# Other places in the order of issue for batches 2 to 8 of a linear-attention and leaky-ReLU kernel

## The chip, the cores and the metric

The kernel runs on one core of a Trainium2 chip. The metric is the device time of one execution in microseconds (us). Times before are the median of three runs; the profile is one further execution, taken by the hardware profiler.

## The reference

For each of 8 batches and 8 heads, with 576 positions of 64 features, `phi(x)` is `relu(x)` times a cosine and times a sine of the position, side by side (128 features). Then

```
kv  = phi(k)^T v            z   = sum over positions of phi(k)
num = phi(q) kv             den = phi(q) z + 1e-6
attn = num / den            x   = attn as (4608 tokens, 512)
h   = x @ w_in              (512 x 2048)
out = max(0.01 h, h) @ w_out    (2048 x 512)
```

Inputs and output are float32.

## The kernel before

**Groups.** 512 of a batch's 576 positions form one group of rows; the last 64 of all eight batches together form a ninth group. So there are groups 0 to 8, each with 512 rows, and each goes through attention and both layers. Operands of matmuls are float16, sums float32.

**Attention of a group.** `loads(b, 0/1/2)` bring q, k and v by SyncE's queue into staging buffers (pool `stage`, three buffers). `k_part`, `q_part` and `v_part` convert them on VectorE (DVE) or ScalarE (ACT): index `j` is a quarter of the rows (4 is the tail of 64), the next index is 0 for cosine and 1 for sine. `kv_all(b)` makes phi(k)^T v with 36 small matmuls and a copy on ACT; it reads `vmain` (from `v_part(b, 0)` for heads 0 to 3 and `v_part(b, 1)` for heads 4 to 7) and `vtail` (`v_part(b, 2)`). `q_transpose_dma(b, j)` transposes a quarter of phi(q) by a DMA. `num(b, j)` multiplies it with kv into the one buffer `ps_num` of its pool, and DVE divides by `den` into `xs`. `x_transpose_dma(b, j)` turns `xs` into a quarter of `xT` by a DMA; for group 2 alone `x_transpose(2, j)` does it on TensorE (PE), and ACT copies the result.

**Layers by seven products.** From group 1's second layer and group 2's first layer on, a 2 x 2 block product is made from seven block products instead of eight (Strassen's scheme). `x_sums(g, s)` makes the sums of blocks of `xT` that these need (tile `xw`): s = 1 gives `xw[0]`, s = 2 `xw[1]` (which product 6 reads), s = 3 and 4 the rest. `w1_sums` and `w2_sums` do so for the weights. `p1(g, t, n, ...)` is product n of row tile t in the first layer, four matmuls with 256 columns; `p2(g, n, pair, u, ...)` is one of the second layer, also four matmuls. Between products, ACT copies sums in PSUM from bank to bank (`seed`), ACT and DVE gather results (`u_copy`, `u_add`), and ACT applies the leaky ReLU (`lrelu`, `u_lrelu`). `g_sums(g, n, lo, hi)` makes on DVE the block sums for the second layer, and `o_copy`, `o_add`, `o_store` gather and store its output.

**Order.** The pool scheduler decides nothing here: instructions go to each engine's queue in the order in which the code issues them, and each queue runs strictly in order. From line 1008 on, the code collects steps with a position each in a list `line`, sorts the list by position and issues it. PE's products lie on a regular grid: `f1_stream(g)` places the first layer of group g at `top[g]`, with 58 positions to a group (56 from group 4 on), and `f2_stream(g - 1)` the second layer of the group before beside it, so that both alternate in runs of four matmuls. All other steps are put at positions from tables written out by hand:

- `AT[b]` for the attention of group b (5 stands for 5 to 8; from 4 on relative to `top[b]`), with entries `load`, `kc`, `ks`, `v`, `kv`, `qc`, `qs`, `qt`, `num`, `xt`, `xs`
- `ENG[b]` for the engine of each conversion
- `F1_AT`, `F4_AT`, `F2_AT`, `F24_AT` for the ACT and DVE steps behind each product
- `G1_AT`, `G_AT`, `G3_AT`, `G4_AT`, `GL_AT` for `g_sums`, `W1_AT`, `W2_AT`, `R_AT` for the sums of weights
- `LAST`, `LAG4` for where the last second layers begin

Everything before that (group 0, the attention of group 1, the conversion of the weights) is issued directly, ends near 52 us, and is not touched.

Of the kernel before, what the change touches and what calls it, by code (L numbers as in the profile page):

```python
# [18 lines left out]
def kernel(  # L19
# [60 lines left out]
    ACT, DVE, POOL = nc.scalar, nc.vector, nc.gpsimd  # L80
# [151 lines left out]
    kv = [const.tile([P, H, NE], dt.float16, name=f"kv{b}") for b in range(B)]  # L232
# [574 lines left out]

    SEED, JOIN, ALL = 2, 3, 4

    F1_AT = {'seed': (0.3, 0.7, 0.5), 'u1': (1.0, 1.0, 1.0), '11': (5.3, 1.3, 2.8), 'u2': (0.3, 0.7, 0.5), '22': (1.8, 0.6, 0.2), '21': (0.5, 0.8, 1.9), '12': (0.5, 1.6, 1.1), 'out': (2.7, 2.7, 2.1)}  # L810

    P_AT = (
# [4 lines left out]
    ONE_AT = ((4, 7), (12, 14), (17, 18), (22, 25))  # L817

    P4_AT = {1: 0, 6: 3, 2: 5, 7: 6, 5: 8, 4: 9, 3: 11}
    F4_AT = {'seed': 1.0, 'u1': 4.1, '11': 7.9, 'u2': 7.6, '22': 9.4, '21': 10.3, '12': 11.2, 'out': 12.9}  # L820

    def f1_stream(g):

        evs = [(-0.1, quarters, (g,))]
        for t in range(3 if g < ALL else 4):
# [7 lines left out]
            for n, nm, f, args in (  # L833
# [4 lines left out]
            ):  # L838
                pos_ = at_[n] + F1_AT[nm][t] if g < ALL else 7 * t + F4_AT[nm]
                evs.append((pos_, f, (g, *args)))  # L840
# [76 lines left out]
                o_src[o * TAIL : (o + 1) * TAIL, pairs, cols],  # L917
            )

    F24_AT = {'u0': 2.7, '11': -0.2, 'u1': 1.7, 'u2': -0.7, '22': 0.6, '21': 0.5, '12': 0.0, 'low': 1.9, 'top': 3.1}  # L920
    F2_AT = {'u0': 0.7, '11': -0.7, 'u1': -0.1, 'u2': -0.9, '22': -0.5, '21': -0.1, '12': 0.9, 'low': 2.5, 'top': 3.3}

    def f2_stream(g):

# [3 lines left out]
        for n, bank, fresh in (  # L928
# [7 lines left out]
            for nm, f, args in {  # L936
# [73 lines left out]
    def put(pos, f, *args):  # L1010
        line.append((pos, len(line), f, args))
# [4 lines left out]

    AHEAD, LAG, LAST, LAG4 = 14, 2, 9, 2.5
    length = {g: 58 if g < ALL else 56 for g in range(2, NG)}  # L1020
    top = {2: 2 * NFT + AHEAD}
    for g in range(3, NG + 1):
# [24 lines left out]

    W1_AT = {3: (38.5, 53.5)}  # L1050
# [22 lines left out]
    for i in range(2):  # L1073
        put(W1_AT[3][i], w1_sums, i, 3, 0, 4 - 2 * i)
    for s, at_ in zip((1, 2, 4, 3), R_AT):
        put(top[ALL - 1] + at_, w1_sums, 1, s, 2, 4)
    for s, at_ in W2_AT.items():
        for i in range(2 - len(at_), 2):
            put(at_[i - 2], w2_sums, i, s)
    for s, at_ in G1_AT.items():  # L1080
        for u in range(2):
            put(at_[u], g_sums, 1, s, 4 * u, 4 * u + 4)
    for g in range(2, NG):
        which = GL_AT if g == NG - 1 else G_AT if g < ALL - 1 else G3_AT if g < ALL else G4_AT
        for s, at_ in which.items():
# [58 lines left out]
```

## Time and profile before

| what | value |
|---|---|
| median of three runs | 271.71 us (271.64 to 272.72) |
| the profiled execution, device time | 272.88 us |
| its span, first to last instruction | 271.0 us |
| matmuls | 2660 |
| busy: PE, DVE, ACT | 263.2, 201.6, 200.8 us |
| granted TensorE clock | 0.999 |
| DMA: bytes moved, mean rate | 57.05 MB, 211 GB/s |
| last matmul ends | 267.4 us |

The busy times are shares of one execution. PE is matmul time and PEld is the time of loading weights, which runs beside it; the ends of matmuls are modelled, so the start of one to the start of the next is the better measure of what a matmul takes. A row of a timeline has the start in us, the time, the engine, the line, the operation and the tiles; "x4" says that four instructions stand in one row, and a bracket how long the engine was idle before and for whom it waited. All steps of one helper have one line, so a row is told by its tiles and its place in time.

### The profile page before, as it was taken

The numbers are of one execution on the slowest core, as the hardware profiler recorded it, in microseconds if no ns is written. First come the engines' busy times: TensorE is split into PE (matmuls) and PEld (weight loads), VectorE is DVE, ScalarE is ACT, GpSimd is POOL, SyncE is SP. The second block draws the span as 40 slices with busy tenths as digits, with TensorE's granted clock in tenths as the row PEclk, the third lists the DMA queues.
The fourth block names the chain that finished last, engine by engine and source line by source line (L and its number), as shares of the span: only waits on it lengthen the run. The fifth ranks groups of instructions, "written<-read, shape, count | busy, mean of one in ns | idle before, by whom it ended". The sixth has DMA issues, their size and how long they took to land.

```text
span 271.0 us, 6597 instructions
## 1 busy us (share of the span) xinstructions
PE 263.2 (97%) x2660; PEld 226.1 (83%) x2660; DVE 201.6 (74%) x445; ACT 200.8 (74%) x330; POOL 10.6 (4%) x21
## 2 busy tenths in 40 slices
PE   7799999999999999999999999999999999999994
PEld 5786455765888989889999999999999889999983
DVE  5774799797986797899779696979577758644652
ACT  6666556696878998798899789978966756766621
POOL 1055101000000000000000000000000000000000
PEclk9999999999999999999999999999999999999999
DMA  6999999998999869998999699969384412200324
GB/s 229 313 355 409 408 350 371 354 241 269 296 225 350 148 189 259 297 189 238 280 261 158 184 273 271 175 208 157 77 135 160 62 41 95 82 0 2 144 50 119
DMA packets 87150, 57.05 MB, mean 211 GB/s; under 512 B 56656, under 2 KB 82256, under 8 KB 86608
## 3 DMA queue, kind: packets, MB, share of 16 engines
q1 hardware_dynamic: 86816, 56.37, 78.8%
q8 instruction: 21, 0.34, 0.5%
q10 hardware_dynamic: 304, 0.26, 0.3%
q14 instruction: 9, 0.07, 0.1%
HBM read 36.70 MB, written 9.44 MB: 170 GB/s over the span
## 4 chain that ended last, share of the span: by engine, by line
PE 89%; DVE 4%; DMA 3%; ACT 3%; issue 1%; SPq 0%; DVEq 0%; ACTq 0%
PE ps_o L882 33%; PE ps_h L777 29%; PE ps_h L454 5%; PE ps_h L490 5%; PE ps_o L470 5%; PE ps_h L882 3%; PE ps_num L375 3%; DMA kst<-in_k_dram 3%; PE ps_kv L291 2%; ACT g L751 1%; DVE kpm L240 1%; DVE xp L391 1%; PE ps_qt L365 1%; PE ps_kvh L291 1%; PE ps_numh L411 1%
## 5 line engine op out<-in xcount | busy, mean ns | idle before, releaser
L882 PEld LDWEIGHTS <-g 128*128 128x128 f16 x640 | 62.5, 98 | 7.3 <-DVE g L251 0.2
L251 DVE TENSOR_TENSOR u<-ps_h,u 128x512 f32<-128x512 f32 x52 | 35.8, 688 | 25.2 <-PE ps_h L777 22.3
L882 PE MATMUL ps_o<-w,g 128*128 128x256 f16 x352 | 51.2, 273 | 0.0
L777 PEld LDWEIGHTS <-w 128*128 128x128 f16 x416 | 44.4, 114 | 1.2
L777 PE MATMUL ps_h<-xT,w 128*128 128x256 f16 x288 | 43.3, 273 | 0.0
L804 ACT ACTIVATE g<-u 128x1024 f16<-128x1024 f32 x26 | 27.5, 1057 | 10.9 <-DVE u L251 10.8
L777 PEld LDWEIGHTS <-wa 128*128 128x128 f16 x312 | 34.0, 113 | 1.7 <-DVE xw L254 0.6
L790 ACT ACTIVATE g<-ps_h 128x512 f16<-128x512 f32 x52 | 31.2, 602 | 5.7 <-PE ps_h L777 5.7
L797 ACT COPY u<-ps_h 128x512 f32<-128x512 f32 x52 | 30.4, 585 | 5.5 <-PE ps_h L777 5.4
L882 PE MATMUL ps_o<-wb,g 128*128 128x256 f16 x232 | 33.5, 273 | 0.0
L777 PE MATMUL ps_h<-xw,wa 128*128 128x256 f16 x208 | 31.3, 273 | 0.3 <-DVE xw L254 0.3
L882 PEld LDWEIGHTS <-gs 128*128 128x128 f16 x256 | 24.9, 98 | 2.9
L900 ACT COPY ob<-ps_o 128x512 f32<-128x512 f32 (+1 forms) x32 | 17.9, 561 | 9.2 <-PE ps_o L882 9.0
L490 PE MATMUL ps_h<-xT,w 128*128 128x512 f16 (+1 forms) x104 | 24.7, 363 | 0.0
L391 DVE TENSOR_TENSOR xs<-ps_num,rden 128x512 f16<-128x512 f32 x28 | 19.3, 691 | 1.0
L882 PE MATMUL ps_o<-w,gs 128*128 128x256 f16 x120 | 17.8, 273 | 0.0
L251 DVE TENSOR_TENSOR ob<-ps_o,ob 128x512 f32<-128x512 f32 (+1 forms) x22 | 14.8, 674 | 3.7 <-ACT ob L900 1.4
L254 DVE TENSOR_TENSOR gs<-g 128x1024 f16<-128x1024 f16 x16 | 11.0, 688 | 8.8 <-ACT g L804 8.7
L882 PE MATMUL ps_o<-wb,gs 128*128 128x256 f16 x120 | 17.5, 273 | 0.0
L787 ACT COPY ps_h<-ps_h 128x512 f32<-128x512 f32 x26 | 14.9, 572 | 2.3 <-PE ps_h L777 1.5
L777 PE MATMUL ps_h<-xT,wa 128*128 128x256 f16 x104 | 15.6, 273 | 0.0
L777 PE MATMUL ps_h<-xw,w 128*128 128x256 f16 x104 | 15.6, 273 | 0.0
(112 smaller groups left out, 412.3 us busy)
## 6 DMA issues: line engine op xcount, KB each, us to landing
qst<-in_q_dram SPq DMA_DIRECT2D x7, 1024.0 KB, 6.3
out_dram<-ob SPq DMA_DIRECT2D x14, 512.0 KB, 2.8
kst<-in_k_dram SPq DMA_DIRECT2D x6, 1024.0 KB, 8.0
vst<-in_v_dram SPq DMA_DIRECT2D x6, 1024.0 KB, 7.5
w1st<-in_moe_w_in_dram SPq DMA_DIRECT2D x8, 512.0 KB, 9.9
w2st<-in_moe_w_out_dram SPq DMA_DIRECT2D x4, 1024.0 KB, 13.4
kst<-in_k_dram SPq DMA_DIRECT2D x4, 512.0 KB, 7.5
vst<-in_v_dram SPq DMA_DIRECT2D x4, 512.0 KB, 7.9
```

The lines of the kernel that those rows point to most:

```text
L251: nc.vector.tensor_tensor(out=o, in0=a, in1=b, op=ALU.add)
L391: nc.vector.tensor_tensor(out=xs, in0=ps[:, :, 0 : 4 * NE].rearrange("p a (b e) -> p a b e", e=NE)[:, :, :, 0:D], in1=rden.rearrange("p (a ...
L454: nc.tensor.matmul(ps[:, m % 2, lo:hi], lhsT=w1[m // 4][c // 2][:, c % 2, m % 4 : 512 : 4], rhs=xT[:, c, lo:hi], start=(c == 0 and lo == 0 ...
L470: nc.tensor.matmul(ps, lhsT=st["g", g][:, m, tt * P : (tt + 1) * P], rhs=w2[:, m, :], start=(m == 0), stop=(m == NFT - 1),)
L490: nc.tensor.matmul(ps[:, lo:hi], lhsT=w1[m // 4][c // 2][:, c % 2, m % 4 : 512 : 4], rhs=st["xT", g][:, c, lo:hi], start=(c == 0 and lo == 0),
L777: nc.tensor.matmul(bank[:, p], lhsT=w(c), rhs=st["xb", g][n][:, c], start=(fresh and p == 0 and c == 0), stop=(c == 1), skip_group_check=True,
L787: nc.scalar.copy(bank1[bj], bank1[bi])
L790: nc.scalar.activation(st["g" + nm, g][:, 2 * t : 2 * t + 2], bank1[bi], AF.Lrelu)
L797: nc.scalar.copy(st["u", g, t][:, n], bank1[bi])
L804: nc.scalar.activation(st["gt", g][:, :, 1, 2 * t : 2 * t + 2], st["u", g, t], AF.Lrelu)
L882: nc.tensor.matmul(bank, lhsT=st[G2[n], g][:, m, pair * P : (pair + 1) * P], rhs=W2[n](m), start=(fresh and m == 0), stop=(m == NH - 1), s ...
L900: nc.scalar.copy(o_at(g, half_, col, pair), bank_of(bi, pair, pair is None))
```

## The change

The change gives other numbers to the tables named above, and nothing else. The products on PE keep their grid. What moves are the steps of batches 2 to 8 among them (conversions, loads, transposes, `num`, `x_sums`, `g_sums`, the sums of weights, the ACT and DVE steps behind each product), and which of DVE and ACT does a conversion. The second layer of the last groups begins half a unit (`LAG4`) or one position (`LAST`) later. In the diff, each entry of a table stands on a line of its own, and entries that the text does not speak of are left out.

```diff
 F1_AT = {
-  'seed': (0.3, 0.7, 0.5), '11': (5.3, 1.3, 2.8), '21': (0.5, 0.8, 1.9), 'out': (2.7, 2.7, 2.1)
+  'seed': (0.6, 0.5, 1.1), '11': (3.5, 0.2, 3.1), '21': (0.3, 1.4, 1.6), 'out': (2.1, 2.1, 2.4)
...
-AHEAD, LAG, LAST, LAG4 = 14, 2, 9, 2.5
+AHEAD, LAG, LAST, LAG4 = 14, 2, 10, 3
...
-W1_AT = {3: (38.5, 53.5)}
+W1_AT = {3: (51.0, 51.5)}
...
-G_AT = {3: (-6.5, 10.5), 2: (0.0, 11.0), 1: (17.5, 32.5), 4: (23.0, 29.5)}
+G_AT = {3: (-5.5, 11.0), 2: (10.5, 21.0), 1: (15.5, 33.0), 4: (25.0, 23.5)}
...
 ENG = {2:
-  'kc': (DVE, DVE, DVE, DVE, DVE), 'ks': (ACT, DVE, DVE, ACT, DVE), 'v': (ACT, DVE, ACT)
+  'kc': (ACT, ACT, DVE, DVE, DVE), 'ks': (DVE, DVE, DVE, DVE, DVE), 'v': (DVE, DVE, ACT)
...
 AT = {2:
-  'kc': (-12.0, -0.5, 13.0, 5.5, 13.0), 'ks': (-22.5, -12.5, -17.0, -10.5, 1.0), 'v': (8.0, 11.0, 13.0)
+  'kc': (-12.0, -4.0, -0.5, 2.5, 7.0), 'ks': (-35.5, -23.5, -37.0, -32.5, -13.0), 'v': (6.0, 9.0, 13.0)
-  'qc': (-8.5, 2.5, 4.5, 9.0), 'qs': (0.0, 4.5, 7.5, 13.0), 'qt': (6.0, 7.0, 8.0, 14.0)
+  'qc': (-23.0, -8.5, -1.5, 0.0), 'qs': (-4.5, 0.0, -1.5, 10.0), 'qt': (-1.5, 6.5, 14.5, 19.0)
-  'kv': (16.5,), 'num': (19.0, 20.5, 24.0, 27.5), 'xt': (24.4, 24.9, 26.9, 30.9)
+  'kv': (17.5,), 'num': (19.0, 21.0, 24.0, 27.5), 'xt': (24.4, 25.4, 28.4, 30.9)
...
 3:
-  'load': (20.5, 24.0, 32.0), 'qc': (26.0, 29.0, 31.0, 36.5), 'xs': (102.5, 106.0, 104.5, 114.0)
+  'load': (19.0, 23.5, 29.5), 'qc': (27.5, 29.0, 32.0, 40.5), 'xs': (103.0, 103.5, 106.5, 117.5)
...
 5:
-  'num': (-37.0, -32.3, -19.6, -15.9), 'xt': (-24.5, -17.8, -17.6, -6.9), 'xs': (-2.5, -1.5, -1.5, 16.0)
+  'num': (-37.0, -31.8, -17.6, -12.4), 'xt': (-29.5, -21.3, -5.1, -2.9), 'xs': (-2.5, 3.0, 5.5, 16.0)
...
```

More of the change, by code (lines that the diff above doesn't have):

```diff
@@ L808 @@
     SEED, JOIN, ALL = 2, 3, 4
-    F1_AT = {'seed': (0.3, 0.7, 0.5), 'u1': (1.0, 1.0, 1.0), '11': (5.3, 1.3, 2.8), 'u2': (0.3, 0.7, 0.5), '22': (1.8, 0.6, 0.2), '21': (0.5, 0.8, 1.9), '12': (0.5, 1.6, 1.1), 'out': (2.7, 2.7, 2.1)}
+    F1_AT = {'seed': (0.6, 0.5, 1.1), 'u1': (0.5, 1.0, 1.0), '11': (3.5, 0.2, 3.1), 'u2': (0.3, 0.6, 0.5), '22': (2.4, 0.2, 0.5), '21': (0.3, 1.4, 1.6), '12': (0.5, 1.6, 1.1), 'out': (2.1, 2.1, 2.4)}
     P_AT = (
@@ L819 @@
     P4_AT = {1: 0, 6: 3, 2: 5, 7: 6, 5: 8, 4: 9, 3: 11}
-    F4_AT = {'seed': 1.0, 'u1': 4.1, '11': 7.9, 'u2': 7.6, '22': 9.4, '21': 10.3, '12': 11.2, 'out': 12.9}
+    F4_AT = {'seed': 0.7, 'u1': 4.6, '11': 5.5, 'u2': 6.5, '22': 9.3, '21': 11.0, '12': 11.5, 'out': 12.7}
     def f1_stream(g):
@@ L918, in o_store_tail @@
             )
-    F24_AT = {'u0': 2.7, '11': -0.2, 'u1': 1.7, 'u2': -0.7, '22': 0.6, '21': 0.5, '12': 0.0, 'low': 1.9, 'top': 3.1}
-    F2_AT = {'u0': 0.7, '11': -0.7, 'u1': -0.1, 'u2': -0.9, '22': -0.5, '21': -0.1, '12': 0.9, 'low': 2.5, 'top': 3.3}
+    F24_AT = {'u0': 2.0, '11': 0.4, 'u1': 0.0, 'u2': -0.6, '22': 1.4, '21': 0.0, '12': 0.3, 'low': 4.6, 'top': 4.1}
+    F2_AT = {'u0': 2.0, '11': 0.1, 'u1': -0.6, 'u2': -0.7, '22': -0.2, '21': -0.1, '12': 1.0, 'low': 3.5, 'top': 3.3}
     def f2_stream(g):
@@ new lines @@
+    W1_AT = {3: (51.0, 51.5)}
+    W2_AT = {2: (29.5,), 3: (27.0, 16.5), 4: (57.5,)}
+    G1_AT = {3: (18.0, 31.0), 2: (19.5, 36.5), 1: (37.0, 44.5), 4: (66.5, 50.0)}
+    G_AT = {3: (-5.5, 11.0), 2: (10.5, 21.0), 1: (15.5, 33.0), 4: (25.0, 23.5)}
+    G3_AT = {3: (3.5, 12.0), 2: (5.0, 16.0), 1: (11.5, 25.5), 4: (21.5, 48.5)}
+    G4_AT = {3: (-3.0, 17.0), 2: (15.0, 18.5), 1: (27.5, 30.5), 4: (27.5, 51.0)}
+    GL_AT = {3: (-15.5, 14.0), 2: (-0.5, 14.5), 1: (6.0, 16.2), 4: (17.5, 30.0)}
+    R_AT = (35.0, 36.5, 52.5, 46.5)
@@ new lines @@
+    ENG = {2: {'kc': (ACT, ACT, DVE, DVE, DVE), 'ks': (DVE, DVE, DVE, DVE, DVE), 'v': (DVE, DVE, ACT), 'qc': (DVE, DVE, DVE, DVE), 'qs': (DVE, DVE, DVE, DVE)}, 3: {'kc': (ACT, DVE, ACT, DVE, ACT), 'ks': (DVE, ACT, ACT, ACT, ACT), 'v': (DVE, DVE, DVE), 'qc': (ACT, DVE, DVE, ACT), 'qs': (DVE, DVE, DVE, ACT)}, 4: {'kc': (ACT, ACT, DVE, ACT, DVE), 'ks': (DVE, DVE, ACT, DVE, ACT), 'v': (DVE, DVE, DVE), 'qc': (DVE, DVE, ACT, ACT), 'qs': (DVE, ACT, ACT, DVE)}, 5: {'kc': (ACT, DVE, DVE, ACT, ACT), 'ks': (ACT, DVE, DVE, DVE, DVE), 'v': (DVE, DVE, ACT), 'qc': (ACT, DVE, DVE, DVE), 'qs': (ACT, ACT, DVE, ACT)}}
@@ new lines @@
+    AT = {2: {'kc': (-12.0, -4.0, -0.5, 2.5, 7.0), 'ks': (-35.5, -23.5, -37.0, -32.5, -13.0), 'v': (6.0, 9.0, 13.0), 'kv': (17.5,), 'qc': (-23.0, -8.5, -1.5, 0.0), 'qs': (-4.5, 0.0, -1.5, 10.0), 'qt': (-1.5, 6.5, 14.5, 19.0), 'num': (19.0, 21.0, 24.0, 27.5), 'xt': (24.4, 25.4, 28.4, 30.9), 'xs': (37.5, 48.0, 41.5, 55.5)}, 3: {'load': (19.0, 23.5, 29.5), 'kc': (50.5, 50.5, 55.0, 57.0, 55.0), 'ks': (31.0, 42.0, 55.0, 49.5, 45.0), 'v': (53.5, 60.5, 50.5), 'kv': (62.0,), 'qc': (27.5, 29.0, 32.0, 40.5), 'qs': (30.0, 29.0, 34.0, 41.5), 'qt': (31.5, 39.5, 40.0, 46.5), 'num': (69.5, 76.5, 82.5, 88.0), 'xt': (87.0, 88.0, 93.5, 96.0), 'xs': (103.0, 103.5, 106.5, 117.5)}, 4: {'load': (-82.0, -110.0, -109.5), 'kc': (-71.5, -59.0, -52.0, -73.5, -55.5), 'ks': (-69.5, -54.0, -75.0, -57.5, -52.0), 'v': (-81.0, -40.5, -39.0), 'kv': (-37.0,), 'qc': (-74.0, -66.5, -50.5, -40.5), 'qs': (-71.0, -52.5, -45.0, -39.0), 'qt': (-49.5, -37.5, -32.5, -31.0), 'num': (-35.5, -28.8, -23.1, -15.4), 'xt': (-15.0, -9.3, -8.1, -6.4), 'xs': (-2.0, 2.0, 10.5, 17.5)}, 5: {'load': (-101.5, -86.0, -79.0), 'kc': (-66.0, -75.5, -76.5, -53.5, -47.5), 'ks': (-70.5, -60.5, -70.5, -65.0, -70.5), 'v': (-61.0, -54.5, -58.0), 'kv': (-46.0,), 'qc': (-84.5, -81.0, -47.5, -46.5), 'qs': (-74.0, -74.0, -42.0, -29.0), 'qt': (-63.5, -52.0, -37.5, -27.0), 'num': (-37.0, -31.8, -17.6, -12.4), 'xt': (-29.5, -21.3, -5.1, -2.9), 'xs': (-2.5, 3.0, 5.5, 16.0)}}
```

8 lines of the change are left out of this document (removed).

## The prediction

> **What bounds the kernel now.** I read the page first, then the stage windows, then the timelines of the engines round each place where TensorE loses time, and last the order of issue of both kernels beside these rows.
>
> ```profile
> PE 263.2 (97%) x2660; PEld 226.1 (83%) x2660; DVE 201.6 (74%) x445; ACT 200.8 (74%) x330; POOL 10.6 (4%) x21
> ...
> PE 89%; DVE 4%; DMA 3%; ACT 3%; issue 1%; SPq 0%; DVEq 0%; ACTq 0%
> ```
>
> TensorE is busy for 97% of the span and is 89% of the chain that ended last. The windows (span, then busy us per engine) show how little it idles in the part that the change touches, which begins near 52 us:
>
> ```profile
> 52.00:70.00 18.00, 17.48 (x166) 11.50 (x164) 16.06 (x39) 14.56 (x21) 0.00 (x0) 1.00 1.04 283
> 70.00:97.00 27.00, 27.00 (x281) 24.08 (x280) 22.15 (x51) 22.95 (x40) 0.00 (x0) 1.00 1.01 248
> 97.00:125.00 28.00, 27.72 (x286) 24.47 (x284) 24.28 (x54) 24.49 (x44) 0.00 (x0) 1.00 0.96 232
> 125.00:210.00 85.00, 85.00 (x922) 80.76 (x920) 66.97 (x141) 71.58 (x121) 0.00 (x0) 1.00 0.90 196
> ```
>
> From 70 to 97 and from 125 to 210 it never stops. The matmul ends are modelled, so I measure losses by starts: four 256-column matmuls start 0.44 us apart from the next four, a 512-column one takes 0.216, eight of the small `kv_all` ones 0.26. PE's timeline:
>
> ```profile
> 58.81 0.42 PE L291 MATMUL ps_kv<-vmain,kpm 128*128 128x65 f16 x8
> 59.30 0.22 PE L298 MATMUL ps_kv<-vtail,kpt 128*128 128x130 f16 x1
> 59.36 0.42 PE L291 MATMUL ps_kv<-vmain,kpm 128*128 128x65 f16 x8
> 59.61 0.22 PE L298 MATMUL ps_kv<-vtail,kpt 128*128 128x130 f16 x1
> ...
> 61.42 1.03 PE L490 MATMUL ps_h<-xT,w 128*128 128x512 f16 x4
> 62.89 0.41 PE L375 MATMUL ps_num<-kv,qpT 128*128 128x65 f16 x8 [0.45 <-DVE xs L391]
> ```
>
> Place A: the first eight of `kv_all(2)` take 0.49 us to the next step instead of 0.25, a loss of 0.23; the step waits for `vtail`, which ScalarE ends at 59.25. Place N: 61.42 plus 4 x 0.216 is 62.28, the next start is 62.89, a loss of 0.61: `num(2, 1)` needs the one `ps_num` buffer, which VectorE's division for `num(2, 0)` holds to 62.75. Place B is at 97 us: four matmuls start at 96.75, the next at 97.63 instead of 97.19, a loss of 0.44. VectorE's timeline there says why:
>
> ```profile
> 95.88 0.41 DVE L254 TENSOR_TENSOR xw<-xT 128x512 f16<-128x512 f16 x1
> 96.22 0.69 DVE L254 TENSOR_TENSOR gs<-g,gs 128x1024 f16<-128x1024 f16 x1
> 96.82 0.42 DVE L254 TENSOR_TENSOR x<-xT 128x512 f16<-128x512 f16 x1
> 97.15 0.42 DVE L254 TENSOR_TENSOR xw<-xT,xw 128x512 f16<-128x512 f16 x1
> ```
>
> The fourth row is `x_sums(3, 2)`; PE's product 6 of batch 3 waits for its end at 97.57. A, N and B add to 1.28 us, and I find no other place after 52 us that loses over 0.15. So a better order can give at most some 1.3 us, while a worse one has no such floor.
>
> **The change, part by part.** The work is the same: 2660 matmuls, the same 52 DMA transposes, and the same loads and stores. About 40 of 473 runs of matmuls on PE change places with neighbours; on ACT some 30% and on DVE some 40% of the steps move. Of the conversions, DVE has 34 for k instead of 40, 33 for q instead of 29 and 14 for v instead of 8, and ACT the rest. `num(2, 0)` and `num(2, 1)` stand as before, so the 0.61 at N stays.
>
> Place A. `v_part(2, 0)` leaves ACT ahead of `vtail` (a step of 0.94 to the next start), so `vtail` ends near 58.3 instead of 59.25. It lands on DVE, which now runs 13 conversions of 512 columns, two of 256 and `v_part(2, 0)` before `v_part(2, 1)`. Starts in the trace are 0.396, 0.262 and 0.60 apart:
>
> ```profile
> 53.18 0.48 DVE L240 TENSOR_SCALAR kpm<-kst,cos_t 128x512 f16<-128x512 f32 x1
> 53.58 0.48 DVE L240 TENSOR_SCALAR qp<-qst,cos_t 128x512 f16<-128x512 f32 x1
> ```
>
> From 52.38, where DVE's queue for batch 2 begins, that is 13 x 0.396 + 2 x 0.262 + 0.60 = 6.27, so `v_part(2, 1)` runs from 58.65 to 59.34. PE wants it for the second four heads at 59.67 less the lost 0.23, 59.44. It just fits: gain 0.2 (0.23 at best; a loss of 0.2 if DVE is one conversion later). [...]
>
> Place B. `x_sums(3, 2)` now stands directly behind `x_sums(3, 1)`; `g_sums(2, 2)` (0.60) and `x_sums(3, 3)` (0.33) come later. It starts when the first has ended, at 96.36 instead of 97.15, and ends at 96.78, 0.4 before PE's 97.19. Gain 0.44 (0.3 if the chain ahead of it, ScalarE's `u_lrelu` at 93.56, comes a step later).
>
> Place C, the new wait. On SyncE's queue the load of q for batch 3 stands behind the four q transposes of batch 2:
>
> ```profile
> 54.91 6.29 SPq L346 DMA_TRANSPOSE qpT<-qp  x4
> 61.30 0.54 SPq L93 DMA_DIRECT2D qst<-in_q_dram  x1
> ```
>
> ```profile
> qst<-in_q_dram SPq DMA_DIRECT2D x1, 1024.0 KB, 5.7
> ```
>
> It lands at 61.30 + 5.74 = 67.04, and ACT uses it at once:
>
> ```profile
> 66.64 1.02 ACT L751 ACTIVATE g<-ps_h 128x1024 f16<-128x1024 f32 x1
> 67.56 0.71 ACT L238 ACTIVATE qp<-qst,cos_t 128x512 f16<-128x512 f32 x1
> 68.17 0.58 ACT L441 COPY xT<-ps_xt 128x512 f16<-128x512 f16 x1
> ```
>
> The second row, `q_part(3, 0, 0)`, waits for that load. Behind it is the copy of `x_transpose(2, 2)`, and PE's first product of batch 1's second layer needs the buffer that this copy empties; PE starts it at 68.96, 0.2 us after the copy's end at 68.75. In the changed order `q_part(2, 0, 1)` is the eighth step on DVE instead of the sixth, and ends at 55.50, not 54.85. The first transpose, and with it all behind on SyncE, moves by 0.65: load at 61.95, landing at 67.69. `q_part(3, 0, 0)` runs from 67.7, the copy from 68.36 to 68.95; PE, 0.2 earlier through A, wants to go at 68.76. Loss 0.25. It is 0 if the transposes catch up (the first two are 2.35 apart, the rest 1.35); with a landing time of 8.0, the median of the k loads of the same size, it is 2.5. I take 0.25, since 5.74 is the same load from the same place in the queue.
>
> Place D, batches 5 to 7. `num(b, 3)`, and with it the last transpose of x, passes two runs of four matmuls and so stands 0.87 us later against PE. In the trace that transpose of batch 5 took 4.3 us to land and ended 0.74 us before `x_sums(5, 1)`; for batch 6 it was 3.2 and 0.60. So `x_sums(b, 1)` would start 0.13 and 0.27 late. Behind `x_sums(5, 1)`, at 148.28, now stands `v_part(6, 1)` (0.60) ahead of `x_sums(5, 2)`, which ends at 148.28 + 0.33 + 0.60 + 0.42 = 149.6 (149.16 before); PE's product 6 starts at 150.65, its weights 0.1 sooner. So 0.9 is left, and 0.8 or 0.6 after the late start: cost zero, covered by that. Without the cover every us of longer landing is a us of PE. Bounds: 0, and with a landing of 6.65, the longest among the x transposes, 6.65 - 4.3 - 0.8 = 1.6 in batch 5 and 6.65 - 3.2 - 0.6 = 2.8 in batch 6. I take 0, since the same transposes landed sooner than that in the trace.
>
> The other moved steps (`g_sums`, `w1_sums`, `w2_sums`, `seed`, `lrelu`) run on engines with a quarter of their time free, and in both orders stand before their readers on PE. The tail is the same 3.5 us: last matmul, one addition of 0.42, one store.
>
> Sum: -0.2 - 0.44 + 0.25 + 0 = -0.4. The profiled execution took 272.88 us, 271.0 of it the span; so its like would take 272.5. It lies 1.17 above the median of 271.71 (one of the three runs shown does too, 272.72). Against the median: **271.3 us**.
>
> **The rivals.**
> 1. Slower by the load (C). From a landing of 7.5 us, that is 1.75 over its 5.74, the stall at 69 us reaches 2.0 and decides; at 8.0 it is 2.5: -0.64 + 2.5 = +1.9, 273.6. For it: the k loads took 8.0 in the median. Against it: this very load took 5.74, and the q loads 6.3 in the median.
> 2. Slower by D: the last x transposes of batches 5 and 6 land in 5.4, as the one before them did in batch 6: stalls of 0.3 and 1.6, -0.4 + 1.9 = +1.5, 273.2; from there it decides. For it: x transposes in those batches took up to 5.0 and more, and `q_transpose_dma(6, 0)` now stands between those of rows 1 and 2 on SyncE, one more transfer beside them. Against it: the last one of each took 4.3 and 3.2.
> [...]
> 4. Faster by over 0.5%: it needs all of A, B and N. N stays unless the division starts earlier, which nothing in the order does. With N gone and C free, -1.3, 270.4. [...]
>
> **How the numbers follow.** 0.5% is 1.36 us, about what a measurement of this kernel can tell from no change. Forecast with C between 0 and 1 us: 0.78. Rival 1: 0.08. Rival 2: 0.08. Rival 3: 0.02, which stays inside 0.5%. Rival 4 or an unseen gain: 0.04. So faster 0.04, same 0.80, slower 0.16. The range runs from 270.8 (C at zero, both gains full, and 0.2 between runs) to 272.7 (C or D costing 1.4 more than forecast, or a median that falls where the 272.72 run fell), and leaves the far ends of rivals 1 and 2 out.
>
> **What would show it.** In the changed profile: the step to `vtail` at 59 us takes 0.26; no wait of `ps_h` for `xw` at 97; the wait for `xs` at 62 stays near 0.6 by starts; a new wait of `ps_o` L882 for ACT's `xT` copy near 69 us, of a few tenths, with `q_part(3, 0, 0)` waiting for the q load. Wrong if that wait is over 1.5 us, if PE waits for `xw` near 150 or 176, or if the page shows PE idle in the windows from 125 to 210.

## The result, and the profile after

The changed kernel takes 274.25 us (273.05 to 276.22, 22 runs); the kernel before, run beside it, 272.41 (271.64 to 274.58, 22 runs). The ratio is 1.0057, with an interval of 1.0038 to 1.0077. Two later measurements of the same unchanged kernel gave 1.0024 (0.9998 to 1.0050) and 1.0041 (1.0012 to 1.0071). So it is slower by 0.24% to 0.57%, some 0.7 to 1.6 us. The forecast was 271.3 us, 0.4 faster than before, in a range from 270.8 to 272.7; the measured median lies 1.55 us above that range. The second of the three intervals reaches down to no change, the other two do not. The profiled execution took 273.3 us, 271.2 of it the span. (The ratios are of undisturbed runs; the medians are over all runs.)

The page of the changed kernel, engines and chain:

```profile
PE 264.5 (98%) x2660; PEld 226.4 (83%) x2660; DVE 204.7 (75%) x450; ACT 193.4 (71%) x325; POOL 10.5 (4%) x21
...
PE 80%; DMA 9%; DVE 6%; ACT 2%; issue 1%; SPq 1%; DVEq 0%; ACTq 0%
```

PE's share of the chain fell from 89% to 80%, and DMA's rose from 3% to 9%: the chain now leaves PE for transfers in places. The same four windows as before:

```profile
52.00:70.00 18.00, 17.55 (x169) 11.80 (x167) 16.36 (x40) 13.68 (x20) 0.00 (x0) 1.00 0.93 275
70.00:97.00 27.00, 26.46 (x275) 23.44 (x273) 21.82 (x49) 22.68 (x41) 0.00 (x0) 1.00 1.07 238
97.00:125.00 28.00, 27.46 (x283) 24.04 (x281) 23.57 (x53) 22.73 (x41) 0.00 (x0) 1.00 1.01 226
125.00:210.00 85.00, 84.88 (x918) 80.24 (x916) 69.21 (x144) 67.22 (x117) 0.00 (x0) 1.00 0.84 196
```

From 70 to 97 and from 125 to 210 PE had never stopped; now it idles 0.54 and 0.12 there, and 0.54 instead of 0.28 from 97 to 125. The waits of PE name who is late (in total, how often, the longest):

```profile
PE ps_num L375 <- DVE xs L391: 1.0, 2, 0.5
PE ps_h L777 <- DVE xw L254: 0.3, 1, 0.3
...
PE ps_h L777 <- DVE u L251: 0.2, 1, 0.2
```

By starts, as in the prediction, I find these losses after 40 us (each is the step from one start to the next less what the matmuls of that step take):

| place, us | what PE waits for | before | after |
|---|---|---|---|
| 51 | a transpose of batch 1, not touched | 0.26 | 0.26 |
| A, 59 | `v_part(2, 2)` | 0.23 | 0 |
| N, 62 | division of `num(2, 0)` | 0.61 | 0.61 |
| 66 | division of `num(2, 2)` | 0.08 | 0.17 |
| E, 88 | division of `num(3, 2)` | 0 | 0.71 |
| B, 97 | `x_sums(3, 2)` | 0.44 | 0 |
| D in batch 4, 122 to 128 | `u_add(3, 2, 1, 3)`, `x_sums(4, 2)`, `x_sums(4, 3)` | 0 | 0.36 + 0.50 + 0.19 |
| D in batch 5, 150 | `x_sums(5, 2)` | 0 | 0.26 |
| sum | | 1.62 | 3.06 |

The sum grew by 1.44, but the span only by 0.2: in the first 40 us, which the change doesn't touch, PE lost 3.60 us in this execution and 4.82 in the profiled one of before. Over all profiles of this study that part lay between 4.3 and 5.3 for kernels made from before, and between 3.6 and 5.8 for those made from the changed one. It moves an execution by more than the change does, so I read the places, and take the times from many runs.

**Place E.** VectorE, then PE, round 88 us:

```profile
85.04 0.69 DVE L391 TENSOR_TENSOR xs<-ps_num,rden 128x512 f16<-128x512 f32 x1
87.43 0.69 DVE L248 CAST vmain<-vst 128x1024 f16<-128x1024 f32 x1 [1.70 <-DMA vst<-in_v_dram]
88.03 0.16 DVE L386 TENSOR_SCALAR den<-ps_num 128x8 f32<-128x8 f32 x1
```

```profile
88.16 0.60 PE L777 MATMUL ps_h<-xT,w 128*128 128x256 f16 x4
89.30 0.41 PE L375 MATMUL ps_num<-kv,qpT 128*128 128x65 f16 x8 [0.54 <-DVE xs L391]
```

The second row is `v_part(4, 0)`. It stands at the head of VectorE's queue and waits 1.70 us for the load of v of batch 4, which the change puts behind the load of k; the load landed at 87.40 (83.80 before). Behind it stands the division for `num(3, 2)`, whose buffer PE needs for `num(3, 3)`: four matmuls start at 88.16, the next step at 89.30 instead of 88.60.

**Place D, batch 4.** SyncE's queue of the changed kernel, then of the one before, at the x transposes of batch 4:

```profile
113.25 3.99 SPq L357 DMA_TRANSPOSE xT<-xs  x3
117.33 2.09 SPq L346 DMA_TRANSPOSE qpT<-qp  x1
119.51 1.22 SPq L357 DMA_TRANSPOSE xT<-xs  x1
```

```profile
113.40 5.29 SPq L357 DMA_TRANSPOSE xT<-xs  x4
118.78 3.21 SPq L346 DMA_TRANSPOSE qpT<-qp  x2
```

`q_transpose_dma(5, 0)` now stands ahead of `x_transpose_dma(4, 3)`, which is issued at 119.51 and lands at 121.95 (117.47 and 121.18 before). VectorE and PE:

```profile
119.76 0.48 DVE L240 TENSOR_SCALAR kpm<-kst,sin_t 128x512 f16<-128x512 f32 x1
122.07 0.42 DVE L254 TENSOR_TENSOR xw<-xT 128x512 f16<-128x512 f16 x1 [1.83 <-DMA xT<-xs]
122.41 0.68 DVE L251 TENSOR_TENSOR u<-ps_h,u 128x512 f32<-128x512 f32 x1
123.01 0.68 DVE L248 CAST vmain<-vst 128x1024 f16<-128x1024 f32 x1
123.61 0.42 DVE L254 TENSOR_TENSOR xw<-xT,xw 128x512 f16<-128x512 f16 x1
```

```profile
122.35 0.60 PE L882 MATMUL ps_o<-w,g 128*128 128x256 f16 x4
123.15 0.60 PE L777 MATMUL ps_h<-xT,wa 128*128 128x256 f16 x4 [0.20 <-DVE u L251]
124.09 0.63 PE L777 MATMUL ps_h<-xw,wa 128*128 128x256 f16 x4 [0.34 <-DVE xw L254]
```

`x_sums(4, 1)` waits 1.83 us for the transpose. Behind it stand `u_add(3, 2, 1, 3)` and `v_part(5, 1)`, and only then `x_sums(4, 2)`. PE wants the `u_add` at 122.79 and gets on at 123.15; it wants `x_sums(4, 2)` at 123.59 and starts at 124.09. From the landing of x(4, 3), the transpose of the last quarter, to PE's product 6 it is 2.14 us of VectorE's queue.

**Place D, batch 5.** VectorE round 150 us:

```profile
149.46 0.43 DVE L254 TENSOR_TENSOR xw<-xT 128x512 f16<-128x512 f16 x1 [0.98 <-DMA xT<-xs]
149.80 0.69 DVE L248 CAST vmain<-vst 128x1024 f16<-128x1024 f32 x1
150.40 0.42 DVE L254 TENSOR_TENSOR xw<-xT,xw 128x512 f16<-128x512 f16 x1
```

The rows are `x_sums(5, 1)`, `v_part(6, 1)` and `x_sums(5, 2)`. PE wants the last one at 150.62 and starts at 150.88. `x_transpose_dma(5, 3)` is issued at 146.14 and lands at 149.34, against 143.27 and 147.54 before, while PE wanted this product at 150.65 then: the transpose lands 1.80 us later and PE stands where it stood. Ahead of it on SyncE, `q_transpose_dma(6, 0)` took 2.70 us.

### The profile page after: what moved, and what is told of

Its sections match the earlier page's. It is cut to its first block, busy times and chain, and to the rows that moved or that the text cites. A ratio compares the mean times of both kernels' runs of the same rounds, so it can differ in the third digit from the quotient of the medians.

```text
span 271.2 us, 6626 instructions
## 1 busy us (share of the span) xinstructions
PE 264.5 (98%) x2660; PEld 226.4 (83%) x2660; DVE 204.7 (75%) x450; ACT 193.4 (71%) x325; POOL 10.5 (4%) x21
## 4 chain that ended last, share of the span: by engine, by line
PE 80%; DMA 9%; DVE 6%; ACT 2%; issue 1%; SPq 1%; DVEq 0%; ACTq 0%
PE ps_o L882 28%; PE ps_h L777 25%; PE ps_h L454 5%; PE ps_h L490 5%; PE ps_o L470 5%; DMA kst<-in_k_dram 5%; DMA vst<-in_v_dram 3%; PE ps_h L882 3%; PE ps_num L375 2%; PE ps_kv L291 2%; DVE kpm L240 1%; DMA xT<-xs 1%; ACT kpm L238 1%; DVE vmain L248 1%; DVE xp L391 1%
## 5 line engine op out<-in xcount | busy, mean ns | idle before, releaser
L882 PE MATMUL ps_o<-w,g 128*128 128x256 f16 x352 | 50.5, 273 | 0.0
L777 PEld LDWEIGHTS <-w 128*128 128x128 f16 x416 | 45.5, 113 | 1.6 <-DVE xT L254 0.3
L882 PE MATMUL ps_o<-wb,g 128*128 128x256 f16 x232 | 34.3, 273 | 0.0
```

Source lines behind the costliest of these rows:

```text
L777: nc.tensor.matmul(bank[:, p], lhsT=w(c), rhs=st["xb", g][n][:, c], start=(fresh and p == 0 and c == 0), stop=(c == 1), skip_group_check=True,
L882: nc.tensor.matmul(bank, lhsT=st[G2[n], g][:, m, pair * P : (pair + 1) * P], rhs=W2[n](m), start=(fresh and m == 0), stop=(m == NH - 1), s ...
```

## The experiments

Theory Q: a step of VectorE that waits for a transfer stands at the head of its queue and holds up what PE needs. Rival P: PE's other interleaving, or the other split between VectorE and ScalarE, costs the time. Rival S: the difference lies in the first 50 us.

**The changed kernel again, and two numbers back.** `again` has no edit, `v_first` the first edit below, `qt_back` the second, `both_back` both.

```diff
-4: 'load': (-82.0, -110.0, -109.5)
+4: 'load': (-76.5, -104.5, -111.0)
```

```diff
-5: 'qt': (-63.5, -52.0, -37.5, -27.0)
+5: 'qt': (-55.0, -52.0, -37.5, -27.0)
```

> The changed kernel itself once more, to see which of its new PE stalls return. Theory Q (a step of DVE that waits for a DMA stands at the head of DVE's queue and holds up what PE needs behind it): the same three places stall again, near 88.5 us (0.7), 122 to 128 us (0.36 + 0.50 + 0.19) and 150.5 us (0.26), each within 0.5 us of that, and the ratio to the kernel before is again 1.004 to 1.008. Rival P (PE's other interleaving and the other split of conversions over DVE and ACT cost the time): the places differ from run to run while the ratio stays. Rival S (the difference comes from the first 50 us, where the loads of the start vary): the first 50 us of the profile differ by more than the stalls behind.

> The changed kernel with one edit: the loads of batch 4 stand at their old positions, v ahead of k. Theory Q: v lands near 84 us instead of 87.4, v_part(4, 0) does not hold DVE, the PE stall near 88.5 (0.71) is gone, the stalls at 122 to 128 and 150 stay: 0.7 us less than the changed kernel, ratio to before about 1.003. Rival P: the stall stays within 0.2 of 0.7, ratio 1.0055.

> The changed kernel with one other edit: q_transpose_dma(b, 0) of batches 5 to 8 back at its old position (-55.0), so that on SyncE it stands behind the last x transpose of the batch before. Theory Q: x_transpose_dma(4, 3) is issued 1 to 2 us sooner (119.5 in the changed kernel), DVE's wait for it at 122 (1.83) falls under 0.6, and the stalls at 122 to 128 (1.05) and 150 (0.26) fall to 0.3 or less in sum; 88.5 stays: about 1.0 us less, ratio about 1.002. Rival P: the three stalls stay, ratio 1.0055. A third way (the later num(4, 3) alone sets the transposes): the issue moves by under 0.5 us and half of the stalls stay.

> Both edits together. Theory Q: only the wait for the one ps_num buffer near 61 us (0.61, and 0.17 at 65) is left after 52 us, while the two waits that the change took away (0.23 at 59, 0.44 at 97) stay away: 1.7 to 2.0 us less than the changed kernel and 0.2 to 0.5 less than the kernel before, ratio 0.998 to 0.999. Rival P: ratio 1.004 or more.

Measured: `again` 1.0024 (0.9998 to 1.0050), `v_first` 1.0060 (1.0038 to 1.0081), `qt_back` 0.9994 (0.9970 to 1.0019), `both_back` 0.9990 (0.9967 to 1.0013). Losses by starts: `again` 0.35 at E and 0.82 at D; `v_first` none at E, but 0.19 at C, 0.22 at 96 and 1.69 + 0.50 at D; `qt_back` none at E or D; `both_back` none at E or D, 0.26 at C. At E no kernel with the load at its old place loses anything; with the load at the changed place the loss is 0.71, 0.35 and 0 in three profiles of the changed kernel (the third is `again2`, below) and 0 in `qt_back`. So the load's place makes the loss possible, and how late it lands sets its size. The loss at D goes with the q transpose's place, and the larger part of the time goes with D: in `v_first` the loss at E went as theory Q expected, but the time stayed at 1.0060 where Q expected 1.003, as D cost more. `qt_back` has PE's grid and the split of the changed kernel at no loss, which speaks against P. In `qt_back` all four x transposes go out in one row, and the q transposes behind them:

```profile
112.34 6.09 SPq L357 DMA_TRANSPOSE xT<-xs  x4
118.52 2.62 SPq L346 DMA_TRANSPOSE qpT<-qp  x2
```

**One part of the change in the kernel before.** Three kernels, with one edit each in the kernel before:

```diff
-5: 'qt': (-55.0,          b_qt
+5: 'qt': (-63.5,
-4: 'load': (-76.5, -104.5, -111.0)          b_load
+4: 'load': (-82.0, -110.0, -109.5)
-3: 'xs': (102.5, 106.0, 104.5, 114.0)          b_xs
+3: 'xs': (103.0, 103.5, 106.5, 117.5)
```

> The kernel before with one number of the change: AT[5]['qt'][0] from -55.0 to -63.5, so that q_transpose_dma(5..8, 0) stands ahead of the last x_transpose_dma of the batch before on SyncE; nothing else on PE, ACT, POOL or SyncE changes place. Theory Q (a late x transpose holds up VectorE, and VectorE PE): x(4,3), issued at 117.5 in the profile of before, comes one transpose issue (1.35 us) later, near 118.8, and lands near 121.3 instead of 120; x_sums(4,1) waits for it and a stall of 0.2 to 0.5 us appears at p1(4,0,6) near 122; none near 150, where 1.35 us is covered. Total +0.2 to +0.5 us, 1.001 to 1.002. Rival P (PE's other interleaving is the cause): no stall there, 1.000.

> The kernel before with one part of the change: AT[4]['load'] as changed, so that k of batch 4 is loaded ahead of v; nothing else changes place. Theory Q: v of batch 4 lands near 87.4 instead of 83.8, v_part(4,0) idles at the head of VectorE's queue for 1 to 2 us, the division for num(3,2) behind it comes late, and num(3,3) near 88 to 90 loses 0.3 to 0.7 us: 1.001 to 1.0025. Rival P: nothing at 88, 1.000.

> The kernel before with one part of the change: AT[3]['xs'] as changed, so that x_sums(3,2) stands directly behind x_sums(3,1) on VectorE, ahead of g_sums(2,2) and x_sums(3,3). By the prediction's place B: the loss of 0.44 us at p1(3,0,6) near 97 is gone, no new one comes: 0.9985 (-0.4 us). Rival: the stall only moves to a later reader of g_sums or x_sums(3,3), 1.000.

Measured: `b_qt` 1.0003 (0.9970 to 1.0036), `b_load` 0.9991 (0.9960 to 1.0022), `b_xs` 0.9986 (0.9957 to 1.0014); none can be told from no change. By starts, `b_qt` has no loss at 122 to 128, although x(4, 3) landed at 122.18: theory Q missed, the queue place alone is not enough. `b_load` has 0.09 at E, not 0.3 to 0.7:

```profile
88.34 0.69 DVE L248 CAST vmain<-vst 128x1024 f16<-128x1024 f32 x1 [0.84 <-DMA vst<-in_v_dram]
88.95 0.16 DVE L386 TENSOR_SCALAR den<-ps_num 128x8 f32<-128x8 f32 x1
```

VectorE has a sum of weights of 0.6 ahead of this step there, and so idles 0.84 instead of 1.70. And `b_xs` takes the wait for `x_sums(3, 2)` away, but PE gains almost nothing by it:

```profile
97.19 0.60 PE L882 MATMUL ps_o<-w,g 128*128 128x256 f16 x4
97.80 0.60 PE L777 MATMUL ps_h<-xw,wa 128*128 128x256 f16 x4
98.23 0.60 PE L882 MATMUL ps_o<-w,g 128*128 128x256 f16 x4
98.93 0.59 PE L490 MATMUL ps_h<-xT,w 128*128 128x512 f16 x2
```

The steps are 0.61 instead of 0.44 (a loss of 0.17; `seed` on ACT ends at 97.74) and 0.70 (0.26; an `lrelu` on ACT ends at 98.88): 0.43 in place of 0.44. ACT was next in line: two conversions, 0.61 apart, stand right ahead of that `seed`, and in the changed kernel none does.

**Both halves of D in the kernel before; the cost doubled; a candidate.** `b_qt_xs4` is `b_qt` with `4: 'xs'` as changed (first two numbers -2.0 and 2.0 for -0.5 and 0.0). `a_qt2` is the changed kernel with a second q transpose moved ahead of the last x transpose. `cand` is `qt_back` with `v_part(4, 0)` behind the division for `num(3, 2)`. `again2` is the changed kernel.

```diff
-5: 'qt': (-63.5, -52.0, -37.5, -27.0)          a_qt2
+5: 'qt': (-63.5, -63.4, -37.5, -27.0)
-4: 'v': (-81.0, -40.5, -39.0)          cand, beside qt_back's edit
+4: 'v': (-79.3, -40.5, -39.0)
```

> The kernel before with two numbers lists of the change and no more: AT[5]['qt'][0] = -63.5, as in the run b_qt, and AT[4]['xs'] as changed, so that x_sums(4,1) stands on VectorE ahead of a u_add of batch 3 and x_sums(4,2) behind it. PE, ACT and the conversions are those of before. Theory Q (the queue place of the transpose and the place of its reader on VectorE do it together): x_sums(4,1) now waits at the head of VectorE's queue for x(4,3), VectorE idles there 0.5 to 1.5 us, the u_add behind it is late, and PE loses 0.3 to 0.8 us between 122 and 128: 1.001 to 1.003. Rival P (PE's order or the split between VectorE and ScalarE is needed too): no loss there, 1.000.

> The changed kernel with AT[5]['qt'][1] moved as well, from -52.0 to -63.4, so that two q transposes (rows 0 and 1 of the next batch) stand ahead of the last x transposes of batches 4 to 7 on SyncE instead of one; nothing else changes place but one number's moves. The suspected cost doubled. Theory Q: each of those x transposes is issued 1.3 us later than in the changed kernel; the losses of PE near 122 to 128 grow by 1.0 to 1.3 us, those near 150 by about as much, and near 176 up to 1 us appears: +2 to +3.5 us against the changed kernel, 1.010 to 1.017 of before. Rival (the transposes are issued late but VectorE's work ahead of x_sums hides it): under +0.5 us against the changed kernel.

> The changed kernel with AT[5]['qt'][0] back at -55.0 and v_part(4,0) two steps later (AT[4]['v'][0] from -81.0 to -79.3), behind the division for num(3,2) on VectorE. Meant as a version better than both. Theory Q: no idle of VectorE ahead of num(3,2), no loss at 88 whatever the load does, none at 122 to 128 and 150; what is left after 40 us is 0.26 + 0.61 + 0.17 and batch 8, 0.6 under before: 0.998. Rival: the time of a run is set by the first 50 us and the difference can't be seen, 1.000.

> The changed kernel once more, unchanged, beside the three others on one chip, as the mark against which the run with two q transposes is read. Theory Q: losses at 88 of 0.3 to 0.7 and at 122 to 128 of 0.8 to 1.1, 1.002 to 1.006 of before. Rival (the losses of the first profile were chance): sums after 40 us as in before, 1.000.

Measured: `b_qt_xs4` 1.0008 (0.9986 to 1.0030), `a_qt2` 1.0147 (1.0118 to 1.0176), `cand` 1.0014 (0.9997 to 1.0030), `again2` 1.0041 (1.0012 to 1.0071). `again2` loses nothing at E (the load came in time), 0.86 at D in batch 4 and 0.60 in batch 5. In `a_qt2`, VectorE and PE:

```profile
123.48 0.42 DVE L254 TENSOR_TENSOR xw<-xT 128x512 f16<-128x512 f16 x1 [3.51 <-DMA xT<-xs]
```

```profile
122.14 0.60 PE L882 MATMUL ps_o<-w,g 128*128 128x256 f16 x4
124.56 0.60 PE L777 MATMUL ps_h<-xT,wa 128*128 128x256 f16 x4 [1.82 <-DVE u L251]
125.50 1.03 PE L777 MATMUL ps_h<-xw,wa 128*128 128x256 f16 x4 [0.34 <-DVE xw L254]
126.32 1.91 PE L882 MATMUL ps_o<-w,g 128*128 128x256 f16 x8
```

PE loses 1.98 + 0.50 at 122 to 125 (0.86 in the changed kernel) and 1.05 near 153. That is theory Q's dose: the cost grew with the second q transpose put ahead. (In this profile 256-column matmuls start 0.213 us apart instead of 0.109 for 3.3 us behind the stop, which the last section shows; of the six runs, three had a mean granted clock of 0.994, and by the three at 1.000 the ratio is about 1.011.) `b_qt_xs4` shows no loss, against Q's expectation: VectorE idles 0.40 for the transpose, and PE comes later than that. And `cand`, with the q transpose back, did lose 0.70 at D, because its x transposes went out over 7.84 us instead of 6.09 and x(4, 1) alone cost PE 0.31 more. So neither half of D decides by itself.

**The margin.** What decides can be read as one subtraction. Let the margin be the time from the landing of x(4, 3) to PE's product 6 of batch 4 as PE would start it without its waits at 122 to 125. Let the need be the work of VectorE's queue between: with the changed order (`x_sums`, `u_add`, `v_part`, `x_sums`) 121.95 to 124.09, 2.14 us; with the order of before (both `x_sums` together) it is 1.06, from a profile shown below.

| kernel | q transpose ahead | order on VectorE | need | margin | loss at 122 to 125 |
|---|---|---|---|---|---|
| before | no | before | 1.06 | 3.17 | 0 |
| b_qt | yes | before | 1.06 | 2.48 | 0 |
| b_qt_xs4 | yes | changed | 2.14 | 2.47 | 0 |
| qt_back | no | changed | 2.14 | 2.67 | 0 |
| both_back | no | changed | 2.14 | 2.66 | 0 |
| cand | no | changed | 2.14 | 1.44 | 0.70 |
| again | yes | changed | 2.14 | 1.51 | 0.63 |
| again2 | yes | changed | 2.14 | 1.46 | 0.68 |
| after | yes | changed | 2.14 | 1.27 | 0.86 |
| v_first | yes | changed | 2.14 | 0.64 | 1.50 |
| a_qt2 | two | changed | 2.14 | -0.35 | 2.49 |

Where the need binds, the loss is need less margin by construction; what the table adds is that there is none wherever the margin is over the need, and that two things moved. The new order on VectorE doubles the need. And the margin is 1.3 to 1.5 in the changed kernel, against 2.67 in `qt_back` and `both_back`, in `v_first` 2.0 less than there. One profile each stands behind a row, and the q transpose is not alone in setting the margin: without it ahead it was 1.44 in `cand`. Before, the margin was 2.1 us over the need; in the changed kernel it is 0.6 to 0.9 under it. `cand` shows that late transposes alone can do it too, now that the need is 2.14.

**The order on VectorE back.** `xs_back` leaves the q transpose and takes back only where `x_sums` stand; `cand2` takes back the q transpose too and has `cand`'s `v_part(4, 0)`.

```diff
-4: 'xs': (-2.0, 2.0, 10.5, 17.5)    5: 'xs': (-2.5, 3.0, 5.5, 16.0)
+4: 'xs': (-0.5, 0.0, 9.5, 17.0)     5: 'xs': (-2.5, -1.5, -1.5, 16.0)
```

> The changed kernel with the places of x_sums in batches 4 to 8 back (AT[4]['xs'] and AT[5]['xs'] as before), the q transpose left at -63.5; PE, ACT and SyncE as in the changed kernel. On VectorE u_add(3,2,1,3) then comes ahead of x_sums(4,1), and x_sums(b,2) directly behind x_sums(b,1), ahead of v_part. Theory Q2 (the order on VectorE decides: a step that waits for a transpose stands ahead of steps that PE wants sooner): the x transpose still lands near 122, but u_add no longer waits for it and x_sums(4,2) ends near 122.8; the losses at 122 to 128 (0.86 to 1.05 in the three profiles of the changed kernel) and at 150 (0 to 0.6) go to 0.2 or less: 1.000 of before, -1.0 against the changed kernel. Rival (the transpose's late issue decides, wherever its reader stands): at least 0.5 of loss stays near 123, 1.003.

> As xs_back, with AT[5]['qt'][0] back at -55.0 and v_part(4,0) behind the division for num(3,2) on VectorE as in cand. Meant as a version better than both: only the common 0.26, N (0.61) and 0.17 are left after 40 us, as places A and B stay removed. Theory Q2: sum after 40 us 1.0 to 1.1 against 1.6 in before, 0.998. Rival: other transposes or loads that land late make up for it, 1.000.

Measured: `xs_back` 1.0042 (1.0025 to 1.0059), `cand2` 0.9988 (0.9968 to 1.0009). VectorE of `xs_back`:

```profile
122.62 0.43 DVE L254 TENSOR_TENSOR xw<-xT 128x512 f16<-128x512 f16 x1 [1.51 <-DMA xT<-xs]
123.08 0.42 DVE L254 TENSOR_TENSOR xw<-xT,xw 128x512 f16<-128x512 f16 x1
```

x(4, 3) landed at 122.50 and product 6 starts at 123.56, so the need is 1.06. But the margin in this execution was 0.33 (x(4, 0) took 7.4 us to land, 4.8 in the changed kernel's profile), and 0.73 were lost there, then 0.63 each near 127 and 151. Q2's number fell: the order on VectorE alone is no remedy as long as the transpose is late. `cand2`, with both back, has a margin of 1.99 over a need of 1.06 and shows what Q2 expected of it: after 40 us only 0.26, 0.61 and 0.17 are lost, 1.05 in sum where before loses 1.62. In time that can't be told from before: the best version measured, and no proof of a gain.

Over all runs, the kernels of the changed order with the q transpose ahead are at 1.0024, 1.0041, 1.0042, 1.0057 and 1.0060, and those with it back at 0.9988, 0.9990, 0.9994 and 1.0014: the two groups do not overlap, and their means differ by 0.0048, which is 1.3 us. (`a_qt2`, at 1.0147, and `no_store` below, which does less work, at 1.0007, are in neither group.) On the one chip where `again`, `v_first`, `qt_back` and `both_back` ran side by side, the medians were 273.35 and 274.42 us with it ahead, and 272.87 and 273.02 with it back. In the first 40 us PE lost 3.6 to 5.2 us in the profiles of the first group and 3.7 to 5.3 in those of the second, so rival S does not make the difference.

**Two more tries.** `b_num` is the kernel before with `num` and the x transposes of batches 4 to 8 at the changed places; `b_num_qt` has the q transpose there as well. `no_store` is the changed kernel without the two stores of batch 1, so that its output lacks those rows.

```diff
-4: 'num': (-34.0, -28.3, -25.1, -16.4), 'xt': (-19.0, -16.8, -12.1, -6.4)
+4: 'num': (-35.5, -28.8, -23.1, -15.4), 'xt': (-15.0, -9.3, -8.1, -6.4)
-5: 'num': (-37.0, -32.3, -19.6, -15.9), 'xt': (-24.5, -17.8, -17.6, -6.9)
+5: 'num': (-37.0, -31.8, -17.6, -12.4), 'xt': (-29.5, -21.3, -5.1, -2.9)
```

```diff
     def o_store(g, half_):
+        if g == 1:
+            return
```

> The kernel before with the places of num and of the x transposes of batches 4 to 8 as changed (AT[4] and AT[5], 'num' and 'xt') and AT[5]['qt'][0] at -63.5. Theory D2 (the later num and the q transpose ahead of the last x transpose are together the cost): a loss of 0.3 us or more near 122 to 128 or near 150, 1.001 to 1.004. Rival (PE of the kernel before comes to these places 0.7 to 1.4 us later than the changed one, so that the same landing is in time): no loss there, 1.000.

> The kernel before with the places of num and of the x transposes of batches 4 to 8 as changed, the q transpose left at -55.0: place D of the prediction by itself. The prediction: covered, 1.000. Theory D2: a small loss, 0 to 0.3 us, 1.000 to 1.001.

> The changed kernel without the two stores of batch 1's output (512 KB each, issued near 92 and 99 us), so that the output lacks batch 1's rows: 1 MB less for the DMA engines ahead of the x transposes of batch 4. Theory R (the transposes land when the DMA engines, whose share is 0.9 to 1.14 from 97 to 125, come to them): x(4,0) to x(4,3) land 1 us or more sooner than the 118.0 to 122.0 of the changed kernel, and the losses of 0.9 to 1.05 us at 122 to 128 go to under 0.3: 1.000 of before. Rival (SyncE's queue waits for VectorE and ScalarE, not for the DMA engines): they land within 0.4 us of before and the losses stay, 1.004.

Measured: `b_num` 1.0081 (1.0044 to 1.0118), `b_num_qt` 1.0130 (1.0097 to 1.0163), `no_store` 1.0007 (0.9981 to 1.0034). The first two are dearer than the whole change, and not at D in batch 4, where neither lost anything. `b_num` lost 1.73 at `num(6, 3)`, 0.74 at `g_sums(2, 1, 4, 8)` near 111 and 0.54 at two ACT steps near 151; in the changed kernel the steps of VectorE round these places moved along with `num`. `b_num_qt` has the first two as well (1.72 and 0.74), and in place of the third it lost 0.46 at D in batch 5: `x_sums(5, 1)` waited 0.97 for its transpose, and PE for the `u_add` four steps behind. That is what theory D2 had forecast there, but the time of these two runs can't be read for D: one list of such an order, put into another order, makes waits of its own. In `no_store` the stores are gone, but the x transposes of batch 4 landed at 119.02 to 122.98, no sooner than the 118.02 to 121.95 of the changed kernel: a megabyte less ahead of them did not bring them in earlier, so the simple form of theory R falls. It lost less at D (0.36 + 0.19) for another reason: PE had lost 5.77 in its first 40 us, came 2 us later, and so found them landed (margin 1.84). What paces SyncE's queue between 99 and 122, where the changed kernel issues one transfer after another, stays open.

## Why the prediction was wrong, point by point

**A: right.** The step to `vtail` takes 0.26 now (57.91 to 58.17), 0.23 gained; 0.2 was forecast. PE's timeline of the changed kernel, A and N:

```profile
57.91 0.42 PE L291 MATMUL ps_kv<-vmain,kpm 128*128 128x65 f16 x8
58.17 0.22 PE L298 MATMUL ps_kv<-vtail,kpt 128*128 128x130 f16 x1
...
59.97 1.03 PE L490 MATMUL ps_h<-xT,w 128*128 128x512 f16 x4
61.45 0.41 PE L375 MATMUL ps_num<-kv,qpT 128*128 128x65 f16 x8 [0.45 <-DVE xs L391]
```

**N: right.** 59.97 + 0.86 is 60.83, the next start 61.45: 0.61 as before. Whether the 0.61 can go stays open: `a_num`, meant to show it with `num(2, 1)` to `num(2, 3)` one position later and the q transpose back, gave no time.

**B: right in the changed kernel, by luck in its cause.** VectorE's rows at B:

```profile
95.23 0.42 DVE L254 TENSOR_TENSOR xw<-xT 128x512 f16<-128x512 f16 x1
95.68 0.42 DVE L254 TENSOR_TENSOR xw<-xT,xw 128x512 f16<-128x512 f16 x1
...
97.01 0.48 DVE L240 TENSOR_SCALAR kpm<-kst,sin_t 128x512 f16<-128x512 f32 x1
97.41 0.48 DVE L240 TENSOR_SCALAR kpm<-kst,cos_t 128x512 f16<-128x512 f32 x1
```

`x_sums(3, 2)` is done at 96.10, and PE's product 6 starts on time at 96.53. But `b_xs` shows that the move I named is worth 0.01 by itself, since ACT is late at the same place. The trace of before had that: its `seed` ended at 97.30, 0.11 after the 97.19 at which PE wanted to go on. In the changed kernel the `seed` ends at 96.15, with no conversion right ahead of it (ACT is 71% busy, 74% before), which the working didn't count. Rival 3, with its chance of 0.02, was that each conversion on VectorE counts its full duration at A. No run shows that: the last two rows start 0.40 apart for an operation of 0.48, and at A in the changed kernel such conversions follow each other in 0.39 to 0.40 too.

**C: too dear.** ACT at 66 us:

```profile
66.27 0.72 ACT L238 ACTIVATE qp<-qst,cos_t 128x512 f16<-128x512 f32 x1
66.90 0.57 ACT L441 COPY xT<-ps_xt 128x512 f16<-128x512 f16 x1
```

The copy ends at 67.47 and PE goes on at 67.59 without a loss; 0.25 was forecast. The q load of batch 3 was issued 5.61 us after the first q transpose (59.90 less 54.29), not 6.39 as before: the transposes caught up, the case for which the prediction had said 0. In other profiles of the changed order it was 0.19 (`v_first`) and 0.26 (`both_back`), each time with ACT waiting for that load (0.31 and 0.39): mechanism and size were right where the loss came up at all.

**D: the step that failed.** "Cost zero, covered by that" was taken from the cover of the kernel before, and the cover was spent twice. I counted the later `num(b, 3)` and `v_part` ahead of `x_sums(b, 2)` in batches 5 to 7. I did not add the issue of the q transpose, which I had seen standing ahead of the x transpose in the order of issue and put down as a word for rival 2 only. On SyncE it took 2.0 to 3.0 us beside the x transposes of batches 4 and 5 in the three profiles of the changed kernel, and the trace of before had shown that it would not be free: I had written that the q transposes of batch 2 go out 1.35 apart, the first two 2.35. So in the first of these profiles x(5, 3) landed 1.80 us later against PE, not 0.87, and the cover of 0.8 was gone. And I did not look at batch 4, where `x_sums(4, 1)` passed a `u_add` that PE wants sooner. The measured cost is 0.8 to 1.1 us in batch 4 and 0 to 0.6 in batch 5 in the three profiles of the changed kernel (1.7 and 0.5 in `v_first`), where the term was zero. Two signs that the prediction had named for being wrong came: PE waits for `xw` near 150 and idles between 125 and 210. Rival 2 had the right mechanism at a chance of 0.08, but put it in batches 5 and 6; the larger part came in batch 4.

**E: not costed at all.** The swap of the loads of k and v in batch 4 was part of "the same loads and stores". The moved load of v landed 3.6 us later (1.7 of it from its place in the queue, the rest from its time to land, 8.3 us instead of 6.4), and the step that reads it stood at the head of VectorE's queue ahead of a division that PE waits for. It cost 0.71, 0.35 and 0 in the three profiles.

**The level.** Three runs of before with a median of 271.71 were low: beside the changed kernel before took 272.41, and 272.5 to 273.0 later. Some 0.7 us of the distance between 271.3 and 274.25 is this; the rest is the change itself, 1.8 slower where 0.4 faster was forecast.

## What to carry to other kernels

When an order written out by hand changes, price each moved transfer where it is issued: its time on the queue (2.0 to 3.0 us for the q transpose here), what stands behind it there, and who waits at the head of which engine's queue for the thing that now lands later. Read the cover as one subtraction, landing to need, for every batch that the moved number reaches, and spend it once. At B the gain at one wait was worth only the distance to the next engine in line, 0.01 of 0.44 us in `b_xs`: a run with that edit alone shows it.

## What the runs showed of the hardware

In the profile of `a_qt2` a stretch at a lower clock follows the stop of 1.98 us. The windows show:

```profile
122.00:124.50 2.50, 0.74 (x7) 0.53 (x6) 1.02 (x3) 2.09 (x4) 0.00 (x0) 1.00 0.72 248
...
125.40:128.70 3.30, 3.20 (x16) 2.29 (x17) 3.26 (x8) 1.30 (x2) 0.00 (x0) 0.53 0.74 215
128.70:135.00 6.30, 6.30 (x88) 5.99 (x87) 3.99 (x10) 3.48 (x7) 0.00 (x0) 0.98 0.79 206
```

For 3.3 us the granted clock is 0.53, and 256-column matmuls start 0.213 us apart instead of 0.109; that is another 1.6 us lost (estimated as 3.3 x 0.47). Behind the stop of 1.73 us in `b_num` nothing of the kind is seen, and the mean granted clock of that profile is 1.0. Of the six runs of `a_qt2`, three took 277.04 to 277.52 us at a mean granted clock of 0.994, which is what 3.3 us at 0.53 make of a span of 274.9, and three 275.20 to 275.58 at 1.000, some 1.8 us less. The profile is of one of the first three. But a mean of 0.994 is not found in `a_qt2` alone: seven of the runs of before that stood beside the experiments have it too, at 274.10 to 274.72 us. Whether the stop brings the low clock on, these runs do not show.

The first of the four x transposes of batch 4 took 4.7 to 7.9 us from issue to landing (4.7 in `qt_back`, 7.9 in `cand`, where the queue ahead of it has the same order). That scatter is larger than the cost of the change. In the three profiles of the changed kernel it took 4.8 to 5.0, and the loss at 122 to 125 still ran from 0.63 to 0.86. What makes the landing scatter, these runs do not show.
